# An attention and two MLPs: weight tiles of the second MLP converted in another order, one tile a step, and stores of the first MLP's output issued a step later

## The chip, the cores and the metric

The kernel runs on one core of a Trainium2 chip. The metric is the device time of one execution in microseconds; of several runs the median is taken.

## The reference

Three parts follow each other; all numbers are float32, the weights of the MLPs arrive as float64 words.

```python
scores = q @ k.T / 8 + bias(log1p(|i - j|) / log1p(max(i, 1)))   # 4 batches, 8 heads, 576 x 64
x = softmax(scores) @ v                                          # -> 2304 tokens x 512
h = x @ w_in                                                     # 512 x 2048
x2 = (h - tanh(h)) @ w_out                                       # 2048 x 512
gate = 1 / (1 + exp(-(x2 @ w_gate)))                             # 512 x 1536
out = (gate * (x2 @ w_val)) @ w_out2                             # 1536 x 512
```

## The kernel before

**Precision.** PE multiplies in a reduced float32 format. So each operand is split into a high part (ACT, a cast) and a low part (POOL, the difference), and each product is three: high x high, low x high, high x low.

**Weights.** The class `Weights` (lines 454 to 618) brings each weight tile of 128 x 512 from float64 to a split pair. Its stages: `load` (a DMA into `wraw`, two buffers), `scan` (ACT takes the absolute value of the upper words, L535), `make` (DVE joins the words in four operations, L562, L563, L564, L560) and `split` (ACT's cast, L597, and POOL's difference, L592). The tiles after `scan` are called `wu`. The first 32 items, for the first MLP, stay in SBUF. The others, for the second MLP, are stored to `wsc` in DRAM (`store`, L602) from four staging buffers, and loaded again with each use (`feed`, L802).

**The second MLP's tiles.** Its first two products are computed with seven instead of eight products of 2 x 2 blocks, so four weight blocks `u00`, `u01`, `u10`, `u11` of a group (`fp`, six groups of two blocks of hidden columns) give seven left operands: three are blocks, four are made by the sums of L550, L551, L554 and L555, in place. In the list of items each group has four block tiles, then `c0` and `c1` (the sums, two each, and the splits of what they give), then two tiles of the output weight. That is 6 tiles to convert, 4 sums and 9 splits a group.

**The first MLP.** 48 steps, `n`; 6 blocks of 384 tokens, each visited for the first and later for the second half of the hidden columns, four steps a visit. In step `n` PE runs `first(n)` (24 products `up`, L656) and `fifth(n - 2)` (24 down products into four banks `acc`, L720). Between them lie `second` (ACT: two functions of `up`, L673, and a square, L676), `third` (DVE: five operations, L686 to L690, with one of ACT, L685) and `fourth` (ACT's casts `gh`, L694, and POOL's `gl`, L701). Three steps after a visit's last step `sixth` empties the four banks into `o`: by DVE and ACT in the first visit, by four DVE additions (L736) in the second, and stores them to `x2s` (L740); `partial` (L727) reads them back between. The tokens `xm` of the next block are loaded (L640) and split (`x_split`, L646 and L647) in two of four steps.

**How the conversion is placed.** Nothing schedules it: each engine runs its instructions in the order in which the Python writes them. The loop over `n` (lines 964 on) writes ACT's list `acts`, then runs `third`'s operations and a tile's four conversion operations in turn (`zip_run`), then `sixth`, PE's products, the low parts of the splits, and the next `scan`. For items `c0` and `c1`, where `make` gives two operations, the `while` loop goes on:

```python
            if len(made) != 2:
                break
            run()
            for l in low:
                l()
```

so steps 24, 30, 36 and 42 hold both items and the tile after them. `later` puts a DMA off to the next step's `tick` (in the second MLP to the second slot after): the raw loads and the stores of splits, not those of `x2s`. SP issues all DMAs, in order, and waits at each for what it needs.

**The second MLP.** 252 slots `s` of six matmuls (L848), 14 for a group and pair of token blocks; twelve of the 14 also have a down product of three matmuls (L864). Two banks alternate, so slot `s + 2` waits for the evacuation of slot `s` (L892 to L909, ACT or DVE). Slots 0 to 6 stand in the last two steps of the first MLP's pipeline. The rest of the weight tiles is converted between slots by `convert` (lines 808 to 821), with sums on DVE and three staging buffers. Thirteen buffers hold loaded weights; when the first of a group come free, `feed` issues one load or, in every fourteenth slot, seven.

## Time and profile before

| what | value |
|---|---|
| median of 3 runs (1225.12 to 1227.8) | 1226.7 us |
| profiled execution, its time | 1230.97 us |
| profiled execution, its span | 1229.2 us |
| mean granted clock of PE over the span | 0.97 |
| PE busy | 1137.2 us (93%) |
| DVE, ACT, POOL busy | 814.2, 660.2, 622.5 us |
| shares of the chain that ended last | PE 73%, DVE 7%, DMA 6%, issue 5%, POOL 5%, ACT 4% |

The times are those of the core. The span is the stretch that the profile covers; the execution's own time is a little longer. Times in rows are microseconds from the start of the span. A busy PE is not PE at its peak: its ends are modelled, and at a lower granted clock the same matmuls take longer.

### The profile page before, as it was taken

The page shows a single profiled execution, that of the slowest core. Times are in us where ns is not written, and L with a number is a line of the kernel's source. Part 1 is how long each engine was busy: PE and PEld are TensorE (multiplying, and loading weights), DVE is VectorE, ACT ScalarE, POOL GpSimd, SP SyncE. Part 2 cuts the span into 40 slices and gives each one's busy share as a digit, 9 for nine tenths or more (in the row PEclk, how much of TensorE's full clock was granted, in tenths as well). Part 3 has the DMA queues.
Part 4 walks back from the last instruction along what each step waited for, and adds up shares of the span by engine and source line. Part 5 has one row for each costly group of instructions (what it writes and reads, how often), then busy time and mean ns, then how long its engine had stood idle before and what let it go on. Part 6 is the DMA issues. An engine that isn't in the chain of part 4 may idle for free.

```text
span 1229.2 us, 19862 instructions
## 1 busy us (share of the span) xinstructions
PE 1137.2 (93%) x6968; PEld 993.5 (81%) x6968; DVE 814.2 (66%) x1415; ACT 660.2 (54%) x1313; POOL 622.5 (51%) x574
## 2 busy tenths in 40 slices
PE   5679999999999999988898887987899999999998
PEld 1256676667699999988897887976799999999997
DVE  8978888888489889887779778456625332442222
ACT  7977888887576676765566556232324222332222
POOL 1057777776455555585557644254535232452232
PEclk9989999999999999999898989988899999999999
DMA  6655555453113333454655476487765665466352
GB/s 218 234 170 166 153 157 167 144 170 99 54 59 114 121 120 104 155 208 140 234 181 201 129 251 219 155 316 270 294 258 215 257 239 224 155 256 256 155 218 109
DMA packets 103027, 225.65 MB, mean 184 GB/s; under 512 B 12176, under 2 KB 52368, under 8 KB 102928
## 3 DMA queue, kind: packets, MB, share of 16 engines
q1 hardware_dynamic: 102928, 224.38, 52.4%
q8 instruction: 56, 0.92, 0.3%
q14 instruction: 43, 0.35, 0.1%
HBM read 166.26 MB, written 58.08 MB: 183 GB/s over the span
## 4 chain that ended last, share of the span: by engine, by line
PE 73%; DVE 7%; DMA 6%; issue 5%; POOL 5%; ACT 4%; SPq 0%; DVEq 0%; ACTq 0%; POOLq 0%
PE sum L848 19%; PE acc L720 13%; PE up L656 11%; PE acc L864 7%; PE sc L227 6%; PE pv L319 5%; PE pt L269 5%; PE sum L864 3%; DMA wsc<-w 2%; DMA bsc<-e 2%; POOL w L592 2%; PE bt L75 1%; DMA wraw<-in_wv 1%; PE pv L316 1%; ACT z L673 1%
## 5 line engine op out<-in xcount | busy, mean ns | idle before, releaser
L848 PE MATMUL sum<-w,w 128*128 128x384 f32 x1512 | 309.0, 344 | 22.7 <-DVE t L905 12.1
L848 PEld LDWEIGHTS sum<-w,w 128*128 128x128 f32 x1512 | 276.7, 192 | 46.6 <-DVE t L905 13.4
L720 PE MATMUL acc<-gh,w 128*128 128x384 f32 x768 | 203.5, 347 | 27.0 <-DVE o L736 21.1
L656 PE MATMUL up<-xt,w 128*128 128x384 f32 x1152 | 208.7, 335 | 1.8 <-DVE t L690 1.8
L656 PEld LDWEIGHTS up<-xt,w 128*128 128x128 f32 x1152 | 199.9, 188 | 5.2 <-PE acc L720 2.7
L720 PEld LDWEIGHTS acc<-gh,w 128*128 128x128 f32 x768 | 144.1, 196 | 29.9 <-issue 20.3
L701 POOL TENSOR_TENSOR gl<-t,gh 128x384 fp32r<-128x384 f32 x96 | 103.0, 1093 | 127.2 <-issue 57.3
L259 POOL TENSOR_SCALAR n<-n,rec 128x576 f32<-128x576 f32 x144 | 120.8, 853 | 82.1 <-DVE rec L254 47.6
L592 POOL TENSOR_TENSOR w<-wu,w 128x512 fp32r<-128x512 f32 x86 | 124.6, 1456 | 60.4 <-ACT w L597 48.9
L883 POOL TENSOR_TENSOR gl<-e,gh 128x384 fp32r<-128x384 f32 x54 | 57.1, 1059 | 170.8 <-ACT gh L694 170.8
L720 PE MATMUL acc<-gl,w 128*128 128x384 f32 x384 | 132.4, 345 | 2.3 <-POOL gl L701 2.3
L241 DVE CUSTOM_DVE_ANT_0 n<-sc,bias 128x576 f32<-128x576 f32 x144 | 103.7, 752 | 32.9 <-PE sc L227 22.5
L248 ACT ACTIVATE n<-n,mn 128x576 f32<-128x576 f32 x144 | 111.6, 785 | 7.2 <-DVE mn L241 6.7
L864 PE MATMUL acc<-w,gh 128*128 128x512 f32 x288 | 91.4, 398 | 0.0
L694 ACT CAST gh<-t 128x384 fp32r<-128x384 f32 x114 | 56.5, 515 | 62.3 <-POOL t L920 55.7
L686 DVE TENSOR_TENSOR t<-up,t 128x768 f32<-128x768 f32 x48 | 45.9, 955 | 61.8 <-ACT t L673 61.8
L685 ACT ACTIVATE z<-z,c 128x768 f32<-128x768 f32 x48 | 45.1, 940 | 76.1 <-DVE up L684 76.0
L269 PE MATMUL pt<-ident,n 128*128 128x128 f32 x576 | 80.4, 281 | 1.4 <-ACT at L299 1.3
L909 DVE TENSOR_TENSOR e<-sum,e 128x384 f32<-128x384 f32 x72 | 40.0, 556 | 60.3 <-PE sum L848 60.2
L562 DVE TENSOR_SCALAR wu<-wu 128x512 f32<-128x512 f32 x68 | 54.3, 799 | 38.6 <-ACT wu L535 38.5
L319 PE MATMUL pv<-at,vs 128*64 128x320 f32 (+1 forms) x512 | 79.3, 421 | 0.0
L720 PEld LDWEIGHTS acc<-gl,w 128*128 128x128 f32 x384 | 75.1, 196 | 3.3 <-POOL gl L701 3.3
(110 smaller groups left out, 2054.7 us busy)
## 6 DMA issues: line engine op xcount, KB each, us to landing
w<-wsc SPq DMA_DIRECT2D x162, 512.0 KB, 7.7
wsc<-w SPq DMA_DIRECT2D x54, 512.0 KB, 4.7
wraw<-in_wo SPq DMA_DIRECT2D x28, 512.0 KB, 4.2
bsc<-e SPq DMA_DIRECT2D x36, 295.5 KB, 3.1
xm<-xs SPq DMA_DIRECT2D x48, 192.0 KB, 3.1
x2s<-o SPq DMA_DIRECT2D x48, 192.0 KB, 2.0
wraw<-in_wi SPq DMA_DIRECT2D x16, 512.0 KB, 4.7
wraw<-in_wg SPq DMA_DIRECT2D x24, 256.0 KB, 3.0
```

The lines of the kernel that those rows point to most:

```text
L227: T.matmul(sc[u, t][:, hf, 0:288], q[r, 128 * s:128 * s + 128], k[r, o:o + 288], start=(i == 0), stop=(i == 2))
L241: V.tensor_tensor_reduce(n.rearrange("p (a b) -> p a b", a=2), s[:, :, 0:288], bias[t].rearrange("p (a b) -> p a b", a=2), -0.125, 3.0e38, ...
L248: A.activation(n, n, AF.Exp, bias=m, scale=-1.0, accum_out=nsum[u, t // 4][:, t % 4:t % 4 + 1])
L259: G.tensor_scalar(n, n, nrec[u, t // 4][:, t % 4:t % 4 + 1], 1.0, ALU.mult, ALU.mult)
L269: T.transpose(pt[:, i], n[:, o:o + 128], ident)
L319: T.matmul(p[0][64 * a:64 * a + 64, 0:N], v[:, c - 1, a], main[:, c - 1, a * N:a * N + N], start=False, stop=(c == 4))
L592: self.nc.gpsimd.tensor_sub(w[:, 1], x, w[:, 0].bitcast(F32))
L656: T.matmul(p[:, 0:TB], w[:, a, 128 * kt:128 * kt + 128], x[:, c], start=(kt == 0 and i == 0), stop=(kt == 3 and i == 2))
L701: G.tensor_sub(l, x[:, j], h.bitcast(F32))
L720: T.matmul(ac[blk][d][:, 0:TB], w[:, a, 128 * d:128 * d + 128], c, start=(begin and j == 0 and i == 0), stop=(end and j == NPR - 1 and i = ...
L848: T.matmul(p, w[:, a, o:o + 128], x[:, c], start=(fresh and kp == 0 and i == 0), stop=(kp == 1 and i == 2), skip_group_check=True)
L864: T.matmul(sums[3 * t + d], g[:, c], w[:, a], start=(begin and i == 0), stop=(end and i == 2))
```

## The change

The items `c0` and `c1` go. A table `JOBS` gives, for each of the six tiles of a group, one sum at most and the splits that go with its step; `step` returns them together with the tile's conversion, and the loop takes one `step` per step of the first MLP. The blocks come in another order (`u10`, `u00`, `u11`, `u01`), the four sums are other ones (`s = u00 - u10`, `u10 + u11`, `u10 - u00`, `u01 - u00`, in place), with which `s` stands for one product's operand directly. Sums stand behind the step's splits on POOL, in both MLPs. Conversion begins in step 2 instead of 3, pauses in steps 45 to 47 instead of from 44 on, and goes on from slot 8, with one conversion operation a slot. Slots 0 and 1 stand in step 48 and slots 2 to 6 in step 49, before three and four. The stores to `x2s` go through `later`.

```diff
 STAGE1 = (0, 1, 2, 3)
-CONV2 = 21
 X0_AT = N1 - 4
+X0_STEPS = (X0_AT + 1, X0_AT + 2, X0_AT + 3)
 
...
         for fp in range(NFP):
-            for n in range(2):
-                for k in range(2):
-                    self.items.append((f"u{n}{k}", fp, [col(w, DF2, 2 * fp + n, 2 * k, 2) for w in (wg, wv)]))
-            self.items += [("c0", fp, None), ("c1", fp, None)]
-            self.items += [("p", 2 * fp + j, [row(wo2, 2 * fp + j)]) for j in range(2)]
-        self.raws = [i for i, x in enumerate(self.items) if x[2]]
+            for n, k in ((1, 0), (0, 0), (1, 1), (0, 1)):
+                self.items.append((f"u{n}{k}", fp, [col(w, DF2, 2 * fp + n, 2 * k, 2) for w in (wg, wv)]))
+            self.items += [(f"p{j}", fp, [row(wo2, 2 * fp + j)]) for j in range(2)]
         self.n = len(self.items)
...
-    def fresh(self, i):
-        if i >= RES:
-            self.turns += 1
-        return (self.more if i >= RES and self.turns % 5 > 2 else self.stage[1]).tile([128, 512], F32, name="wu")
+    def fresh(self, k):
+        return (self.more if k in ("u10", "u00") else self.stage[1]).tile([128, 512], F32, name="wu")
 
     def scan(self):
         i = self.scanned
-        if i >= self.n or i - self.done > 1 or (self.items[i][2] and i not in self.raw):
+        if i >= self.n or i - (self.done if i < RES else self.made) > 1 or i not in self.raw:
             return
         self.scanned += 1
         k, f, src = self.items[i]
-        if not src:
-            return
-        u = self.fresh(i)
+        u = self.tmp[i] = self.u[k, f] = self.fresh(k)
         self.nc.scalar.activation(u, self.raw[i][:, :, 1].bitcast(F32), AF.Abs)
-        self.tmp[i] = u
-        if k[0] == "u":
-            self.u[k] = u
 
...
-        k, f, src = self.items[i]
-        if k == "c0":
-            self.u["s"] = self.fresh(i)
-            u, M = dict(self.u), self.mix
-            return [lambda: M.tensor_add(u["s"], u["u10"], u["u11"]),
-                    lambda: M.tensor_sub(u["u10"], u["u00"], u["u10"])]
-        if k == "c1":
-            u, M = dict(self.u), self.mix
-            return [lambda: M.tensor_sub(u["u11"], u["s"], u["u00"]),
-                    lambda: M.tensor_sub(u["u01"], u["u01"], u["u11"])]
...
+    def part(self, x, w, low, at=None):
+        def do_low():
+            self.nc.gpsimd.tensor_sub(w[:, 1], x, w[:, 0].bitcast(F32))
+            low()
+        return (lambda: self.nc.scalar.copy(w[:, 0], x)), do_low
+
     def split(self):
         i = self.done
-        if i >= self.made:
+        if i >= min(self.made, RES):
             return [], []
         self.done += 1
-        k, f, src = self.items[i]
-        if k in "io":
-            parts = [(None, self.tmp.pop(i))]
-        elif k == "p":
-            parts = [((f // 2, GROUPS2 + f % 2), self.tmp.pop(i))]
-        else:
-            self.tmp.pop(i, None)
-            u = self.u
-            parts = {"u00": [(1, u.get("u00"))], "u01": [(2, u.get("u01"))], "u10": [], "u11": [(4, u.get("u11"))],
-                     "c0": [(5, u.get("s")), (7, u.get("u10"))], "c1": [(6, u.get("u11")), (3, u.get("u01"))]}[k]
-            parts = [((f, PRODUCTS.index(j)), x) for j, x in parts]
-        highs, lows = [], []
-        for at, x in parts:
-            if at is None:
-                w = self.out[i] = self.slot(i)
-            else:
-                w = self.slot(self.stages[self.staged % len(self.stages)])
-                self.staged += 1
-
-            def low(at=at, x=x, w=w):
-                self.nc.gpsimd.tensor_sub(w[:, 1], x, w[:, 0].bitcast(F32))
-                if at is None:
-                    self.usable += 1
-                else:
-                    self.later(lambda: self.store(at, w))
-            highs.append(lambda x=x, w=w: self.nc.scalar.copy(w[:, 0], x))
-            lows.append(low)
-        return highs, lows
+        w = self.out[i] = self.slot(i)
+
+        def low():
+            self.usable += 1
+        h, l = self.part(self.tmp.pop(i), w, low)
+        return [h], [l]
+
+    def staged_part(self, key, f, j):
+        w = self.slot(self.stages[self.staged % len(self.stages)])
+        self.staged += 1
+        return self.part(self.u[key, f], w, lambda: self.later(lambda: self.store((f, j), w)))
+
+    JOBS = {0: (None, (("u01", 3), ("p1", 8))), 1: (None, ()), 2: (("s", "u00", "u10", "sub"), (("u00", 1),)),
+            3: (("u10", "u10", "u11", "add"), (("u11", 4), ("s", 7))),
+            4: (("u00", "u10", "u00", "sub"), (("u10", 5), ("u01", 2))),
+            5: (("u01", "u01", "u00", "sub"), (("u00", 6), ("p0", 7)))}
+
+    def step(self):
+        i = self.made
+        if i > self.n or self.scanned <= i < self.n:
+            return [], [], [], []
+        if i == self.n:
+            self.made += 1
+        highs, lows = self.split()
+        conv = self.make()
+        if i <= RES:
+            return highs, lows, [], conv
+        fp, k = divmod(i - RES, 6)
+        mix, parts = self.JOBS[k]
+        fp = fp - (k == 0)
+        for key, j in parts:
+            h, l = self.staged_part(key, fp, GROUPS2 + int(key[1]) if key[0] == "p" else PRODUCTS.index(j))
+            highs.append(h)
+            lows.append(l)
+        mixes = []
+        if mix:
+            o, x, y, op = mix
+
+            def run():
+                if o == "s":
+                    self.u[o, fp] = self.fresh(o)
+                getattr(self.nc.gpsimd, "tensor_" + op)(self.u[o, fp], self.u[x, fp], self.u[y, fp])
+            mixes.append(run)
+        return highs, lows, mixes, conv
 
...
-            nc.sync.dma_start(x2s[128 * d:128 * d + 128, TB * b:TB * b + TB], o[:, 0:TB])
+            W.later(lambda d=d, o=o: nc.sync.dma_start(x2s[128 * d:128 * d + 128, TB * b:TB * b + TB], o[:, 0:TB]))
...
-        while W.done < W.n:
-            if W.done < W.made:
-                highs, lows = W.split()
-                for f in highs + lows:
-                    f()
-            ops = W.make()
-            for f in ops:
+        while W.made <= W.n:
+            highs, lows, mixes, conv = W.step()
+            for f in highs + lows:
+                f()
+            for f in conv:
                 f()
                 yield
+            for f in mixes:
+                f()
             W.scan()
-            if not ops:
+            if not conv:
                 yield
...
-        low, scans, conv = [], 0, []
-
-        def run():
-            for f in acts:
-                f()
-            zip_run(vecs, conv)
-            for x in (acts, vecs, conv):
-                x.clear()
-        while 2 <= n < X0_AT:
-            if W.done < W.made and (W.done < RES or n >= CONV2):
-                h, l = W.split()
-                acts += h
-                low += l
-            made = W.make()
-            conv += made
-            scans += 1
-            if len(made) != 2:
-                break
-            run()
-            for l in low:
-                l()
-            low.clear()
-            W.scan()
-        run()
+        low, mixes, conv = [], [], []
+        if 2 <= n < N1 and n not in X0_STEPS:
+            h, low, mixes, conv = W.step()
+            acts += h
+        for f in acts:
+            f()
+        zip_run(vecs, conv)
+        if n == N1:
+            only1.close()
+            ev = st.enter_context(tc.tile_pool(name="p3e", bufs=6))
+            upst.close()
+            one = st.enter_context(tc.tile_pool(name="ps_w", bufs=1, space=PSUM))
+            four = [one.tile([128, 512], F32, name=f"sum{i}") for i in range(4)]
+            banks = [x[:, 0:TB] for x in four[:2]]
+            sums = four[2:]
+            W.stages = RING[RING_SLOTS:]
+            W.lag = 2
+        for _ in range({N1: 2, N1 + 1: 5}.get(n, 0)):
+            slot2(s)
+            s += 1
         for m in due(n - 1, 2):
             if ends(m):
                 sixth(m)
@@ -1000,28 +996,11 @@
             for _ in first(n):
                 if n < 2:
                     yield
-        elif n == N1:
-            only1.close()
-            ev = st.enter_context(tc.tile_pool(name="p3e", bufs=6))
-            upst.close()
-            one = st.enter_context(tc.tile_pool(name="ps_w", bufs=1, space=PSUM))
-            four = [one.tile([128, 512], F32, name=f"sum{i}") for i in range(4)]
-            banks = [x[:, 0:TB] for x in four[:2]]
-            W.stages = RING[RING_SLOTS:]
-            W.mix, W.lag = V, 2
-            for _ in range(3):
-                slot2(s)
-                s += 1
-        elif n == N1 + 1:
-            sums = four[2:]
-            for _ in range(4):
-                slot2(s)
-                s += 1
         for m in due(n, 2):
             fifth(m)
-        for l in low:
+        for l in low + mixes:
             l()
-        for _ in range(scans):
+        if n < N1:
             W.scan()
...
-        for _ in range(2 if s % SLOTS2 in (0, 2, 7) else 1):
+        if s > SLOTS2 // 2:
             next(conv, None)
```

How the instructions move shows in two places. The first is POOL around step 30, a step with a pair of sums; `w` are staging buffers of splits, `gl` the low parts of the first MLP's activation, `xt` those of its tokens. Before, L550 to L555 being sums and L592 splits:

```order
L701 TENSOR_TENSOR gl<-t,gh 128x384 x2
L550 TENSOR_TENSOR wu<-wu 128x512
L551 TENSOR_TENSOR wu<-wu 128x512
L592 TENSOR_TENSOR w_7337<-wu,w_7337 128x512
L554 TENSOR_TENSOR wu<-wu 128x512
L555 TENSOR_TENSOR wu<-wu 128x512
L592 TENSOR_TENSOR w_7360<-wu,w_7360 128x512
L592 TENSOR_TENSOR w_7361<-wu,w_7361 128x512
L592 TENSOR_TENSOR w_7370<-wu,w_7370 128x512
L592 TENSOR_TENSOR w_7371<-wu,w_7371 128x512
L647 TENSOR_TENSOR xt<-xm,xt 128x384 x2
L701 TENSOR_TENSOR gl<-t,gh 128x384 x2
```

and now, L597 being sums and L547 splits (steps 29, 30 and the beginning of 31):

```order
L701 TENSOR_TENSOR gl<-t,gh 128x384 x2
L547 TENSOR_TENSOR w_7267<-wu,w_7267 128x512
L547 TENSOR_TENSOR w_7268<-wu,w_7268 128x512
L597 TENSOR_TENSOR wu<-wu 128x512
L647 TENSOR_TENSOR xt<-xm,xt 128x384 x2
L701 TENSOR_TENSOR gl<-t,gh 128x384 x2
L547 TENSOR_TENSOR w_7364<-wu,w_7364 128x512
L547 TENSOR_TENSOR w_7365<-wu,w_7365 128x512
L597 TENSOR_TENSOR wu<-wu 128x512
L647 TENSOR_TENSOR xt<-xm,xt 128x384 x2
L701 TENSOR_TENSOR gl<-t,gh 128x384 x2
L547 TENSOR_TENSOR w_7469<-wu,w_7469 128x512
```

Four sums and five splits of one step have become one sum and two splits in each of several steps, and every step's `gl` stands ahead of its splits.

The second is SP around slots 13 to 21 of the second MLP, where raw tiles (`wraw`) stand among loads of weights (`w<-wsc`), stores of splits (`wsc<-w`) and loads of the next tokens (`xt<-x2s`). Before, the first pair of raw loads below being issued in slot 15:

```order
L802 DMA w_9291<-wsc_8_81 128x1024
L802 DMA w_9302<-wsc_0_82 128x1024
L802 DMA w_9316<-wsc_1_83 128x1024
L767 DMA xt<-x2s 128x768
L514 DMA wraw<-in_wg 128x2x256
L514 DMA wraw<-in_wv 128x2x256
L767 DMA xt<-x2s 128x768
L602 DMA wsc_2_102<-w_9338 128x1024
L767 DMA xt<-x2s 128x768 x2
L518 DMA wraw<-in_wo 128x1024 x2
L602 DMA wsc_5_105<-w_9433 128x1024
L602 DMA wsc_4_104<-w_9452 128x1024
```

and now, the raw loads being issued in slots 13, 17 and 21:

```order
L802 DMA w_9304<-wsc_8_81 128x1024
L513 DMA wraw<-in_wo 128x1024
L802 DMA w_9325<-wsc_0_82 128x1024
L602 DMA wsc_5_105<-w_9316 128x1024
L602 DMA wsc_3_103<-w_9317 128x1024
L802 DMA w_9341<-wsc_1_83 128x1024
L767 DMA xt<-x2s 128x768 x3
L513 DMA wraw<-in_wo 128x1024
L767 DMA xt<-x2s 128x768
L602 DMA wsc_4_104<-w_9393 128x1024
L602 DMA wsc_2_102<-w_9394 128x1024
L509 DMA wraw<-in_wg 128x2x256
```

The raw load of slot 15 has moved behind two stores of splits and three loads of tokens, to slot 17.

## Rows read from the trace of the kernel before

**Rows 1.** Windows: stretch, us; busy by engine (x); granted clock; DMA share; GB/s.
```profile
345.53:512.61 167.08, 167.08 (x962) 166.26 (x961) 149.83 (x193) 117.89 (x193) 94.19 (x82) 1.00 0.36 111
512.61:764.87 252.26, 221.09 (x1201) 216.57 (x1199) 199.71 (x244) 146.62 (x239) 149.78 (x126) 0.94 0.56 194
787.55:891.61 104.06, 86.29 (x404) 77.83 (x404) 67.39 (x102) 32.55 (x64) 55.50 (x43) 0.89 0.79 294
```

**Rows 2.** Waits of PE after 330 us: sum, times, longest.
```profile
PE acc L720 <- DVE o L736: 21.1, 4, 8.0
PE sum L848 <- DVE t L905: 12.1, 3, 7.1
...
PE sum L848 <- ACT e L892: 3.7, 1, 3.7
```

**Rows 3.** Timeline, step 30: start, us, instruction, count, [idle before <-releaser].
```profile
575.73 1.29 POOL L550 TENSOR_TENSOR wu<-wu 128x512 f32<-128x512 f32 x1
...
582.67 1.36 DVE L563 TENSOR_SCALAR wu<-wu 128x512 int32<-128x512 int32 x1
584.07 1.63 DVE L564 SCALAR_TENSOR_TENSOR wu<-wraw,wu 128x512 int32<-128x512 int32 x1
585.73 1.64 DVE L560 SCALAR_TENSOR_TENSOR wu<-wraw,wu 128x512 int32<-128x512 int32 x1
587.29 1.94 DVE L736 TENSOR_TENSOR o<-acc,o 128x384 f32<-128x384 f32 x4
...
593.37 0.62 ACT L597 CAST w<-wu 128x512 fp32r<-128x512 f32 x1 [11.16 <-DMA wsc<-w]
```

**Rows 4.** Timeline, a step with one conversion and one split.
```profile
449.96 0.81 ACT L673 ACTIVATE z<-up 128x768 f32<-128x768 f32 x1 [0.77 <-PE up L656]
...
452.01 2.17 POOL L701 TENSOR_TENSOR gl<-t,gh 128x384 fp32r<-128x384 f32 x2 [4.61 <-issue]
...
454.14 1.52 POOL L592 TENSOR_TENSOR w<-wu,w 128x512 fp32r<-128x512 f32 x1
...
457.60 1.05 DVE L690 COPY_PREDICATED t<-z,up 128x768 f32<-128x768 int32 x1
```

**Rows 5.** Timeline, a step whose conversion ran beside a POOL busy throughout.
```profile
532.50 0.94 DVE L686 TENSOR_TENSOR t<-up,t 128x768 f32<-128x768 f32 x1
...
533.69 2.40 POOL L701 TENSOR_TENSOR gl<-t,gh 128x384 fp32r<-128x384 f32 x2
...
534.81 0.41 DVE L563 TENSOR_SCALAR wu<-wu 128x512 int32<-128x512 int32 x1
...
536.01 0.68 DVE L564 SCALAR_TENSOR_TENSOR wu<-wraw,wu 128x512 int32<-128x512 int32 x1
...
537.48 0.92 DVE L560 SCALAR_TENSOR_TENSOR wu<-wraw,wu 128x512 int32<-128x512 int32 x1
...
538.32 1.05 DVE L690 COPY_PREDICATED t<-z,up 128x768 f32<-128x768 int32 x1
```

**Rows 6.** Timeline of PE, the up products of steps 46 and 47.
```profile
742.39 4.33 PE L656 MATMUL up<-xt,w 128*128 128x384 f32 x24
...
756.07 1.20 PE L656 MATMUL up<-xt,w 128*128 128x384 f32 x6
```

**Rows 7.** Timeline of ACT in the second MLP: waits on transfers.
```profile
809.19 0.66 ACT L535 ACTIVATE wu<-wraw 128x512 f32<-128x512 f32 x1 [7.23 <-DMA wraw<-in_wv]
...
841.69 0.66 ACT L535 ACTIVATE wu<-wraw 128x512 f32<-128x512 f32 x1 [9.13 <-DMA wraw<-in_wv]
...
878.18 0.62 ACT L597 CAST w<-wu 128x512 fp32r<-128x512 f32 x1 [5.03 <-DMA wsc<-w]
```

**Rows 8.** Timeline of SP there: the burst of weight loads.
```profile
825.42 4.55 SPq L802 DMA_DIRECT2D w<-wsc  x8
```

**Rows 9.** Chain of waits, undisturbed second MLP: start, us, what.
```profile
982.67 3.14 PE sum L848 x18
1005.87 3.14 PE sum L848 x18
```

More of the change, by code (lines that the diff above doesn't have):

```diff
@@ L479, in __init__ @@
         self.stages = STAGE1
-        self.turns = -1
         self.stored = set()
-        self.mix = nc.gpsimd
         self.clock = self.lag = 0
@@ L505, in load @@
     def load(self):
-        if self.loaded >= len(self.raws):
+        i = self.loaded
+        if i >= self.n:
             return
-        i = self.raws[self.loaded]
         self.loaded += 1
```

## The prediction

> **What bounds the kernel now.** I read the windows first, then the waits of PE, then the timeline around the longest waits. PE is the engine to follow: from 345.53 to 512.61 us, the first half of the first MLP, it is busy for all of 167.08 us at a granted clock of 1.00 (2.4 GHz). That is 20 steps, so 8.35 us a step [rows 1] (a row gives PE, PEld, DVE, ACT and POOL in this order). The next 25 steps (up products from step 23, down products to step 45) take 252.26 us where 25 x 8.35 = 208.9 would do: **43.4 us lost**, part of it as idle PE (221.09 busy), part as slower matmuls (clock 0.94). This is the stretch in which tiles of the second MLP are converted. The list of waits names DVE's `o` additions, 21.1 us in four waits, at most 8.0 [rows 2]. In the second MLP 14 undisturbed slots take 1005.87 - 982.67 = 23.20 us; the two slots without a down product take 3.14 / 3 = 1.05 each, the others (23.20 - 2.10) / 12 = 1.76 [rows 9]. Slots 7 to 55 should then take 7 x 1.05 + 3 x 23.20 = 76.9 us and take 104.06 [rows 1]: **27.2 us lost**, around waits for DVE's and ACT's evacuations [rows 2].
>
> The reader is to see in rows 3 how the first loss arises. Step 30 is one of four (24, 30, 36, 42) in which both sums, five splits and the next tile's conversion stand together. POOL starts the first of four sums at 575.73; DVE's conversion of the next tile waits for a scan that stands on ACT behind the casts of the summed tiles, and its four `o` additions, which free the banks of PSUM, begin only at 587.29; ACT's last split waits 11.16 us for a store to leave its staging buffer, since five splits share four buffers and the stores wait in SP's queue behind the `x2s` stores of the same step. DVE is busy for 149.83 of 167.08 us in the plain steps, 7.5 of every 8.35 [rows 1], so a delay of ten microseconds is worked off at about one per step: the four steps disturb nearly all 25.
>
> **The change, part by part.** *Sums and splits spread over six steps.* A group has the same six conversions, nine splits and four sums as before; only their places change. In a crowded step POOL now has two `gl` subtractions (2.17 together [rows 4]), two splits at 1.52 [rows 4] and one sum at 1.29 [rows 3]: 6.5 us of 8.35. In two steps of four two subtractions for x come on top, priced like the `gl` pair: 8.7, over the step. The mean is 2.17 + 1.09 + (9 x 1.52 + 4 x 1.29) / 6 = 6.4 us. POOL therefore falls behind in single steps by less than a microsecond or, where its operations are stretched (2.40 for the `gl` pair beside DVE [rows 5]), by two or three, and recovers in the two light steps of the six. Its deadline is soft: `gl` ends at 454.2, and PE needs it when it comes to those products some 8.35 us after 449.96, four microseconds later.
>
> DVE keeps four conversion operations and five of the activation in each step. In an ordinary step ACT's square starts at 449.96 and DVE ends at 458.65 [rows 4], 8.7 us later; the up buffer is wanted only half a step after that. In every fourth step DVE then adds four `o` (1.94 us [rows 3]), and the next down products wait for the first: 8.7 + 0.5 - 8.35, about 0.9 us, which no order removes. With the crowding I take 1.7 us for each of the four, 7 us. The x products made in steps 45 and 46 stay as they are, and so does their stall: 756.07 - 742.39 - 8.35 = 5.3 us [rows 6]. For a late `gl`, a scan that waits for POOL's sum in the fourth step of six, or a late raw tile I add 3 us. Of the 43.4 us some 15 stay: **28 us gained**.
>
> *Conversions beside POOL.* In the heavy step the last three conversion operations took 1.36 + 1.63 + 1.64 = 4.63 us beside POOL [rows 3]. Between activation operations, with POOL busy without a pause, the same three took 0.41 + 0.68 + 0.92 = 2.01, and DVE's step from 532.50 to 539.37 lasted 6.87 us [rows 5]. The changed steps are of this second kind, so I price them by rows 5; rows 3 are the upper end. The Trainium skill ("SBUF — State Buffer", section "SBUF: two separate sides") speaks against the change here: it says that VectorE and GpSimd lock a shared pair of ports against each other for a whole instruction. By that rule each conversion operation would sit out a subtraction of POOL, and the sum would be that of the slower rival below. The trace agrees in rows 3 and hardly in rows 5, where what DVE does between two conversion operations gives POOL time to end.
>
> *`x2s` stores a step later.* Twelve groups of four stores move past the raw loads, `xm` loads and split stores of one step. Each is now issued when its data is there, so what stands behind it in SP's queue no longer waits for DVE; their buffers are reused four steps later at the earliest, so nobody waits for the later store. What this is worth lies in the 43.4 us and is not counted again.
>
> *Staging.* Two splits a step wrap four buffers after two steps, 16.7 us; a store is issued one step after its split, which leaves it about 8 us to land. ACT's 11.16 us [rows 3] should not come back in the first MLP.
>
> *First slots.* Two and five instead of three and four slots before the last down products: the same matmuls, nothing counted. Bounds: a microsecond either way.
>
> *The second MLP.* Ten tiles instead of twelve are left, one conversion operation a slot, sums on POOL instead of DVE, the raw tile wanted three slots after its issue instead of one to three. What ends the waits there are transfers: ACT waits 7.23 and 9.13 us for raw tiles and 5.03 us for a store [rows 7]. Half-megabyte pieces at the 294 GB/s of that stretch [rows 1] take 1.78 us. Counted from slot 8 (788.6), the raw tile issued in slot 15 of the old order is piece 11.75, done after 20.9 us, at 809.5; the trace has it at 809.19 [rows 7]. In the new order the tile issued in slot 17 is piece 15.75, done after 28.0 us, while its scan stands at the end of slot 20, 6 x 1.05 + 7 x 1.76 = 18.6 us after slot 8. PE has two slots of slack, to 22.1, and resumes at about 30: this wait grows by some 3 us. The burst of seven loads that SP issues from 825.42 on [rows 8] stands in both orders, and the next raw tile is issued behind it in both: the wait of 7.1 us [rows 2] moves by two slots and stays. The third, 3.7 us [rows 2], becomes about 4.7 by the same count, while some waits of under 1 us go. Together: **2 us lost**; between 8 lost, if ACT's splits wait for stores each time, and 14 gained, if one slot more is enough each time.
>
> **Sum.** 28 - 2 = 26 us. The profiled execution took 1231.0 us (span 1229.2), 4.3 over the median of the runs. So 1205 for such an execution and **1201** for the median.
>
> **The rivals.** *The second MLP's waits go as well.* For it: the raw tiles now come evenly, one each four slots, with no slot that takes two operations. Against it: the count of pieces above, and the bursts. 28 + 14 = 42 us gained: 1185.
>
> *POOL's queue becomes the limit in the crowded steps.* For it: 8.7 us of work in single steps, more if stretched. Then `gl` and the scan behind the sum come late, SP waits for the x subtractions before it can load the next raw tile, and I price this at 1 us on 14 of the 24 steps: 1215.
>
> *Slower: POOL holds DVE up in every step.* Place: the zip of activation and conversion, steps 22 to 44. Price: 4.63 - 2.01 = 2.6 us [rows 3, 5] on 6.87 gives 9.5, with a quarter of the additions' 1.94 about 10.0 a step, 1.6 over 8.35; on 24 steps 39 us, against the 38 (43.4 - 5.3) that the spreading can remove, and 2 to 3 lost later: 1230. It decides once DVE's step passes 9.9 us. Against it: rows 5.
>
> *The change does not do what it says.* The heavy wait could reappear at the staging buffers or at SP, and nothing is gained: 1227. Against it: the eight microseconds that each store has.
>
> **How the numbers follow.** Forecast (own range 1191 to 1211, from 22 to 34 us in the first MLP and 8 lost to 4 gained in the second) 0.61; second MLP as well 0.18; POOL 0.13; DVE held up 0.05; nothing 0.03. The range reaches down to the second case and up to the third: 1185 to 1215. Within 0.2% (2.5 us) is about what a measurement of this kernel cannot tell from no change: 0.03 from the last case; slower 0.05; faster 0.92.
>
> **What would show it.** Right: PE takes about 224 us instead of 252 from the up products of step 23 to the end of the down products of step 45; the waits for `o` fall to about 2 us or less each, but one of 3.5 us stays in step 46; no ACT split waits 11 us in the first MLP; POOL is the same in sum. In the second MLP three waits for transfers remain, at other slots. Wrong: conversion operations of 1.4 to 1.7 us in every step (DVE held up), `gl` among the releasers of PE (POOL), or an undisturbed second MLP.

## The result, and the profile after

The changed kernel takes **1192.1 us** (median; 1188.1 to 1192.6), the kernel before, run beside it, 1227.3: a ratio of 0.970, with a 95% interval of 0.967 to 0.974, so 35 us faster. The forecast was 1201 us with a range of 1185 to 1215. The profiled execution of the changed kernel took 1188.1 us (span 1186.0). It is the shortest of its runs, while that of the kernel before was 3.7 us above its median, so the two traces differ by 43 us, eight more than the medians.

Where the 43 us lie, from the windows after (columns as in [rows 1]): up products of step 23 to the end of the down products of step 45, slots 7 to 55, and the first third of those.

```profile
512.72:732.00 219.28, 212.05 (x1201) 210.28 (x1200) 192.76 (x249) 148.57 (x241) 158.33 (x125) 0.98 0.66 227
753.38:848.40 95.02, 81.32 (x404) 72.52 (x404) 61.07 (x86) 30.37 (x60) 64.01 (x50) 0.98 0.83 310
753.40:785.00 31.60, 27.17 (x140) 24.43 (x139) 22.36 (x31) 11.46 (x24) 23.87 (x18) 1.00 0.96 357
```

The 25 steps took 252.26 us [rows 1] and take 219.28: 33.0 us gained, 24.0 of it idle time of PE (31.2 to 7.2) and 9.0 in matmuls that run at a higher granted clock (221.09 busy to 212.05). Slots 7 to 55 took 104.06 and take 95.02: 9.0 gained, 4.1 of it idle time and 5.0 in the matmuls. The last microsecond lies around the handover between the two MLPs. POOL's busy time in the 25 steps, forecast to stay, rises from 149.78 to 158.33; a sum now takes 1.75 us (row of 626.59 below) where it took 1.29 [rows 3].

PE's waits after 330 us (sum, times, longest):

```profile
PE acc L720 <- DVE o L736: 7.2, 5, 4.1
PE sum L848 <- DVE e L909: 4.3, 1, 4.3
PE sum L848 <- issue: 4.2, 1, 4.2
PE sum L848 <- ACT e L892: 3.6, 2, 3.3
PE sum L848 <- DVE t L905: 3.3, 1, 3.3
```

The 21.1 us for `o` [rows 2] have become 7.2, and 4.1 of these are the one wait of step 46 that was to stay. No `gl` of the first MLP is among the releasers. Three waits of the second MLP remain, at 3.3, 4.3 and 3.3 us, where there were 4.5, 7.1 and 3.7. The up products of steps 46 and 47, on PE's timeline, answer to [rows 6]:

```profile
708.28 4.32 PE L656 MATMUL up<-xt,w 128*128 128x384 f32 x24
723.51 1.72 PE L656 MATMUL up<-xt,w 128*128 128x384 f32 x9
```

They begin 15.23 us apart, 6.9 more than a step takes, and more than the 5.3 before.

A crowded step after the change on DVE and POOL (timeline: start, us, instruction, count, [idle before]):

```profile
620.83 0.96 DVE L686 TENSOR_TENSOR t<-up,t 128x768 f32<-128x768 f32 x1 [1.49 <-ACT t L673]
621.71 0.86 DVE L540 TENSOR_SCALAR wu<-wu 128x512 f32<-128x512 f32 x1
622.49 0.95 DVE L687 SCALAR_TENSOR_TENSOR up<-z,up 128x768 f32<-128x768 f32 x1
623.36 0.41 DVE L541 TENSOR_SCALAR wu<-wu 128x512 int32<-128x512 int32 x1
623.69 0.95 DVE L684 SCALAR_TENSOR_TENSOR up<-z,up 128x768 f32<-128x768 f32 x1
624.55 0.92 DVE L542 SCALAR_TENSOR_TENSOR wu<-wraw,wu 128x512 int32<-128x512 int32 x1
625.39 0.95 DVE L689 SCALAR_TENSOR_TENSOR up<-q,up 128x768 f32<-128x768 f32 x1
626.25 0.92 DVE L538 SCALAR_TENSOR_TENSOR wu<-wraw,wu 128x512 int32<-128x512 int32 x1
627.10 1.05 DVE L690 COPY_PREDICATED t<-z,up 128x768 f32<-128x768 int32 x1
...
621.27 2.18 POOL L701 TENSOR_TENSOR gl<-t,gh 128x384 fp32r<-128x384 f32 x2 [1.75 <-ACT gh L694]
623.41 3.21 POOL L547 TENSOR_TENSOR w<-wu,w 128x512 fp32r<-128x512 f32 x2
626.59 1.75 POOL L597 TENSOR_TENSOR wu<-wu 128x512 f32<-128x512 f32 x1
```

POOL is busy from 621.27 to 628.34, and DVE's nine operations take 628.15 - 620.83 = 7.3 us all the same. This is a step of the kind of [rows 5], not of [rows 3].

### The profile page after: what moved, and what is told of

It is laid out like the page before. It is cut to its first block, busy times and chain, and to the rows that moved or that the text cites. A ratio compares the mean times of both kernels' runs of the same rounds, so it can differ in the third digit from the quotient of the medians.

```text
span 1186.0 us, 19853 instructions
## 1 busy us (share of the span) xinstructions
PE 1128.2 (95%) x6968; PEld 982.6 (83%) x6968; DVE 801.4 (68%) x1407; ACT 660.2 (56%) x1313; POOL 644.5 (54%) x582
## 4 chain that ended last, share of the span: by engine, by line
PE 75%; issue 6%; DMA 5%; POOL 5%; ACT 4%; DVE 4%; SPq 0%; DVEq 0%; POOLq 0%; ACTq 0%
PE sum L848 19%; PE acc L720 13%; PE up L656 12%; PE acc L864 7%; PE sc L227 6%; PE pv L319 6%; PE pt L269 6%; PE sum L864 3%; POOL w L547 2%; DMA wsc<-w 2%; DMA bsc<-e 1%; PE pv L316 1%; PE bt L75 1%; ACT y L62 1%; POOL wu L597 1%
## 5 line engine op out<-in xcount | busy, mean ns | idle before, releaser
L848 PE MATMUL sum<-w,w 128*128 128x384 f32 x1512 | 304.4, 341 | 17.3 <-DVE e L909 4.3
L848 PEld LDWEIGHTS sum<-w,w 128*128 128x128 f32 x1512 | 272.3, 189 | 40.8 <-issue 5.1
L720 PE MATMUL acc<-gh,w 128*128 128x384 f32 x768 | 197.9, 338 | 7.3 <-DVE o L736 7.2
L720 PEld LDWEIGHTS acc<-gh,w 128*128 128x128 f32 x768 | 139.7, 190 | 9.8 <-issue 4.4
L547 POOL TENSOR_TENSOR w<-wu,w 128x512 fp32r<-128x512 f32 x86 | 128.2, 1502 | 33.3 <-ACT w L549 33.3
L720 PE MATMUL acc<-gl,w 128*128 128x384 f32 x384 | 129.4, 337 | 0.0
L241 DVE CUSTOM_DVE_ANT_0 n<-sc,bias 128x576 f32<-128x576 f32 x144 | 103.6, 752 | 32.9 <-PE sc L227 23.0
L647 POOL TENSOR_TENSOR xt<-xm,xt 128x384 fp32r<-128x384 f32 x48 | 49.8, 1056 | 45.0 <-ACT xt L646 44.7
L269 PEld LDWEIGHTS pt<-ident,n 128*128 128x128 f32 x576 | 63.4, 141 | 12.5 <-issue 11.5
```

The costliest lines, as they stand in the source:

```text
L241: V.tensor_tensor_reduce(n.rearrange("p (a b) -> p a b", a=2), s[:, :, 0:288], bias[t].rearrange("p (a b) -> p a b", a=2), -0.125, 3.0e38, ...
L269: T.transpose(pt[:, i], n[:, o:o + 128], ident)
L547: self.nc.gpsimd.tensor_sub(w[:, 1], x, w[:, 0].bitcast(F32))
L720: T.matmul(ac[blk][d][:, 0:TB], w[:, a, 128 * d:128 * d + 128], c, start=(begin and j == 0 and i == 0), stop=(end and j == NPR - 1 and i = ...
L848: T.matmul(p, w[:, a, o:o + 128], x[:, c], start=(fresh and kp == 0 and i == 0), stop=(kp == 1 and i == 2), skip_group_check=True)
```

## The experiments

The theory: the heavy steps 24, 30, 36 and 42 make the loss of the first MLP, since in them DVE's conversion waits for a scan that stands behind four sums of POOL, and the `o` additions stand behind that conversion. The first rival: the queue of SP and the staging buffers make it. For the second MLP: the even pace makes the gain, or the sums off DVE, or the smaller number of tiles.

### The stores alone, on the kernel before

```diff
-            nc.sync.dma_start(x2s[...], o[:, 0:TB])
+            W.later(lambda d=d, o=o: nc.sync.dma_start(x2s[...], o[:, 0:TB]))
```

> The kernel before with one part of the change alone: the four output stores of a block are issued a step later. Theory (the bunched sums and splits of steps 24, 30, 36 and 42 make the loss of the first MLP, and the stores are only a side matter): 25 steps from the up products of step 23 to the end of the down products of step 45 still take 247 to 253 us, and the whole 1222 to 1228. Rival (the stores wait in SP's queue for DVE's additions and hold up the split stores and raw loads behind them): the stretch falls to 235 us or less, the whole to 1210 or less, and ACT no longer waits some 11 us for a staging buffer.

Measured: 1227.4 us against 1231.3, ratio 0.997 (0.995 to 0.998); the 25 steps take 249.0 us, as the theory had it.

### Eight staging buffers, on the kernel before

```diff
-STAGE1 = (0, 1, 2, 3)
+STAGE1 = (0, 1, 2, 3, 4, 5, 6, 7)
```

> The kernel before with eight staging buffers in place of four in the first MLP, all else the same, so that five splits of one step never wait for a store. Theory (three things are bunched in a heavy step: four sums on POOL, the scan behind the casts, and the splits that wait for a buffer; the last is a part only): ACT's waits of some 11 us go, the 25 steps take 232 to 245 us instead of 252, the whole 1208 to 1221. Rival 1 (the staging buffers are all of it): 222 us or less and 1198 or less. Rival 2 (they are beside the path): 250 or more and 1225 or more.

Measured: 1228.0 us against 1231.3, ratio 0.998 (0.996 to 0.999); the 25 steps take 248.6 us. Rival 2 was nearer than the theory's figure. In the kernel before, ACT's list of waits in the 25 steps holds this line, two waits of up to 11.2 us:

```profile
ACT w L597 <- DMA wsc<-w: 21.7, 2, 11.2
```

It is gone in this run and in the run with the stores alone. **21.7 us of waiting were taken away, in two ways, and each gave some 3.5 us.** The prediction had shown that wait as a part of what is bunched in a heavy step; it was hardly what PE stood for. What PE stood for is DVE in step 30 of this same run:

```profile
576.14 1.08 DVE L690 COPY_PREDICATED t<-z,up 128x768 f32<-128x768 int32 x1
580.59 0.90 DVE L562 TENSOR_SCALAR wu<-wu 128x512 f32<-128x512 f32 x1 [3.38 <-ACT wu L535]
581.53 1.37 DVE L563 TENSOR_SCALAR wu<-wu 128x512 int32<-128x512 int32 x1
582.94 1.63 DVE L564 SCALAR_TENSOR_TENSOR wu<-wraw,wu 128x512 int32<-128x512 int32 x1
584.60 1.64 DVE L560 SCALAR_TENSOR_TENSOR wu<-wraw,wu 128x512 int32<-128x512 int32 x1
586.16 1.94 DVE L736 TENSOR_TENSOR o<-acc,o 128x384 f32<-128x384 f32 x4
```

The activation is done at 577.2; 3.4 us go by until the scan, then 5.6 us of conversion in a row beside POOL, and only then come the additions, for which PE waits 7.97 us in this run.

### The sums left out, on the kernel before

```diff
-            self.u["s"] = self.fresh(i)
+            self.fresh(i)
+            self.u["s"] = self.u["u11"]
...
-            return [lambda: M.tensor_add(u["s"], u["u10"], u["u11"]),
-                    lambda: M.tensor_sub(u["u10"], u["u00"], u["u10"])]
+            return [lambda: None, lambda: None]
...
-            return [lambda: M.tensor_sub(u["u11"], u["s"], u["u00"]),
-                    lambda: M.tensor_sub(u["u01"], u["u01"], u["u11"])]
+            return [lambda: None, lambda: None]
```

> The kernel before with the four sums of a group left out everywhere (its summed tiles are then not the sums); loads, conversions, splits and stores all stay. Theory (in a heavy step the chain sums on POOL, casts of the summed tiles, scan of the next tile, its conversion on DVE, o additions makes the loss; the stores and the staging buffers gave 3.6 us each): the 25 steps fall from 252 us to 222 to 234, the waits for o to 3 us or less each. Rival (five splits and stores in one step are enough for it): 242 us or more, and o waits of 6 to 8 us stay.

Measured: 1213.0 us against 1229.2, ratio 0.987 (0.984 to 0.990). The 25 steps take 235.8 us, just over what the theory gave, and the longest wait for `o` falls from 8.0 to 3.7, where the theory had 3 or less. So without the sums half of it is gone: 16.5 of the 33.0 us that the change gained there. The other half is left with the five splits and the conversion in one step; which of these two keeps it this run does not tell.

### The next tile a step later, on the kernel before

```diff
             low.clear()
             W.scan()
+            if W.items[W.made - 1][0] == "c1":
+                break
```

> The kernel before, where a heavy step ends behind its sums: the next tile is converted a step later, so that no activation operation on DVE stands behind a conversion that waits for the sums. Everything is still computed, four tiles later in the second MLP. Theory (DVE's wait inside the heavy step makes the loss): the 25 steps take 222 to 236 us, o waits 4 us or less each; the second MLP then loses 5 to 25 us more, with some sixteen tiles left. Rival (the sums and casts delay gh and gl themselves): 242 us or more.

Measured: 1202.0 us against 1229.2, ratio 0.978 (0.976 to 0.981). **The 25 steps take 218.6 us, the same as in the changed kernel (219.3)** and fewer than the theory's 222 to 236. The four sums are still bunched with three of the five splits, the stores stand where they stood, and the last two splits have moved on with the conversion. But groups now take seven steps, so there are three heavy steps instead of four, and fewer tiles are converted in this stretch (18 times L560, where the kernel before has 21 and the changed kernel 22 of the same operation). That the gain does not come from this alone shows in step 38, which is heavy and has additions:

```profile
642.34 1.29 POOL L550 TENSOR_TENSOR wu<-wu 128x512 f32<-128x512 f32 x1
...
643.88 1.06 DVE L690 COPY_PREDICATED t<-z,up 128x768 f32<-128x768 int32 x1
644.84 1.93 DVE L736 TENSOR_TENSOR o<-acc,o 128x384 f32<-128x384 f32 x4
650.63 0.96 DVE L686 TENSOR_TENSOR t<-up,t 128x768 f32<-128x768 f32 x1 [3.86 <-ACT t L673]
```

The sums begin at 642.34, the additions follow the activation at once, DVE then waits 3.86 us with nothing to do, and PE does not wait at all. What made the loss is the conversion that stood between; to move it, with the two splits behind it, is enough. How much of the equality with the changed kernel is owed to the smaller number of tiles is not shown. The price lies behind: 15 tiles instead of 12 are left over, and slots 7 to 55 take 107.1 us instead of 104.1.

### The stores at once, on the changed kernel

```diff
-            W.later(lambda d=d, o=o: nc.sync.dma_start(x2s[...], o[:, 0:TB]))
+            nc.sync.dma_start(x2s[...], o[:, 0:TB])
```

> The changed kernel with the output stores of a block issued at once again. Theory: with the work spread there is slack in SP's queue, so the 25 steps take 219 to 222 us and the whole 1188 to 1196. Rival (the stores a step later carry a good part of the gain): 228 us or more, 1200 or more.

Measured: 1191.4 us, ratio 0.967 (0.965 to 0.970) to the kernel before; the 25 steps take 218.4 us. The later stores are worth nothing here: some 3.5 us on the kernel before, none once the steps are even.

### Conversion behind the activation, on the changed kernel

```diff
-        zip_run(vecs, conv)
+        for f in vecs + conv:
+            f()
```

> The changed kernel with the four conversion operations of a step behind the five of the activation on DVE in the first MLP, instead of between them. It tests what the alternation does for DVE beside a busy POOL. Theory (activation operations that read PSUM in between give POOL time to end its own): the four operations, now in a row, rise from 2.96 us a step to 4 to 6 us, DVE's step passes 8.35 us in crowded steps, and the whole is 1195 to 1215. Rival (the order of the two does not matter): the four stay within 0.4 us of 2.96 us a step and the whole is 1186 to 1193, since the up buffer is then even released earlier.

Measured: **1237.1 us** against 1231.3, ratio 1.0045 (1.002 to 1.007): the whole gain is gone and a little more. Neither account had that. The rival's time is out by 44 us, the theory's by 22, and the four operations rise less than the theory had, to a mean of 3.2 us a step over the first 21 steps (the sum of the means of their four groups, 0.55 + 0.66 + 0.99 + 0.96) and of 3.5 from 534 to 700 us. But a step as a whole, with POOL at work beside it, goes from 7.3 to 8.7 us (548.22 to 556.91):

```profile
548.22 0.96 DVE L686 TENSOR_TENSOR t<-up,t 128x768 f32<-128x768 f32 x1
549.09 0.95 DVE L687 SCALAR_TENSOR_TENSOR up<-z,up 128x768 f32<-128x768 f32 x1
550.08 0.96 DVE L684 SCALAR_TENSOR_TENSOR up<-z,up 128x768 f32<-128x768 f32 x1
551.14 0.96 DVE L689 SCALAR_TENSOR_TENSOR up<-q,up 128x768 f32<-128x768 f32 x1
552.21 1.07 DVE L690 COPY_PREDICATED t<-z,up 128x768 f32<-128x768 int32 x1
553.17 0.41 DVE L540 TENSOR_SCALAR wu<-wu 128x512 f32<-128x512 f32 x1
553.61 1.15 DVE L541 TENSOR_SCALAR wu<-wu 128x512 int32<-128x512 int32 x1
554.80 1.39 DVE L542 SCALAR_TENSOR_TENSOR wu<-wraw,wu 128x512 int32<-128x512 int32 x1
556.22 0.69 DVE L538 SCALAR_TENSOR_TENSOR wu<-wraw,wu 128x512 int32<-128x512 int32 x1
```

8.7 is over the 8.35 of PE, and the emptying of the four banks stands behind it. PE's waits from 345 to 780 us are these:

```profile
PE acc L720 <- DVE o L736: 22.1, 5, 5.3
PE acc L720 <- DVE o L739: 13.7, 6, 3.5
PE acc L720 <- ACT o L739: 2.4, 1, 2.4
```

They make 38.2 us in twelve waits, one for each of eleven emptyings and a second for the first of them, and that is all the idle time of PE in both stretches. It begins ahead of step 23: the stretch from 345.5 us to the up products of step 23 takes 188.5 us instead of 167.2, and the 25 steps 244.5 instead of 219.3. DVE's slack is thin: 1.4 us more a step turn 35 us of gain into a loss. This is the kind of loss that the prediction's slower rival had, a DVE step over 8.35 us. But the step is 8.7 us long and not 10.0, and 21 of the 46 us lost lie ahead of the steps for which the rival was priced. The alternation of the two kinds of operation is what kept it away.

### The additions earlier, on the changed kernel

```diff
+        if n < N1:
+            vecs[3:3] = [lambda m=m: sixth(m) for m in due(n - 1, 2) if ends(m)]
         zip_run(vecs, conv)
...
-        for m in due(n - 1, 2):
-            if ends(m):
-                sixth(m)
+        if n >= N1:
+            for m in due(n - 1, 2):
+                if ends(m):
+                    sixth(m)
```

> The changed kernel with the four o additions of a block issued between the third and the fourth of DVE's activation operations instead of behind the step's conversion. Theory (the additions stand late on DVE, not on its load): PE's waits for o fall from 7.2 to 2 us or less in sum, the 25 steps take 212 to 216 us instead of 219.3, the whole 1182 to 1188. Rival (DVE is full, the wait moves to the up buffer): 218 to 221 us, with waits for L690.

Measured: 1187.9 us, ratio 0.968 (0.966 to 0.970); the 25 steps take 216.5 us. The four waits of 0.6 to 1.2 us are gone. The wait of step 46 went from 4.1 to 2.9 us, but another of 2.8 us has come up a step later, for a `gh` cast of step 45. That is half a microsecond more than the theory gave at most, and less than the rival. As slots 7 to 55 take 97.9 us in this trace, the whole is not clearly shorter than that of the changed kernel.

### The second MLP: sums, pace and number

```diff
+        self.mix = nc.gpsimd
...
-                getattr(self.nc.gpsimd, "tensor_" + op)(...)
+                getattr(self.mix, "tensor_" + op)(...)
...
-            W.lag = 2
+            W.mix, W.lag = V, 2
```

> The changed kernel with the sums of the second MLP on DVE, as before, instead of POOL. Slots 7 to 55 take 94.9 us in the changed kernel and 103.9 in the kernel before. Theory (the 9 us come from the even pace, which leaves each raw tile three slots to land): 94 to 97 us, the whole 1187 to 1194. Rival (DVE freed of the sums makes them): 100 us or more, the whole 1196 or more.

```diff
-        if s > SLOTS2 // 2:
+        for _ in range(2 if s % SLOTS2 in (0, 2, 7) else 1):
             next(conv, None)
```

> The changed kernel with the pace of the old one in the second MLP: conversions begin in slot 7 and slots 0, 2 and 7 of each fourteen take two operations. Theory (the even pace makes the 9 us of the second MLP): slots 7 to 55 take 99 to 105 us instead of 94.9, the whole 1192 to 1203, with longer waits of ACT for raw tiles. Rival (ten tiles instead of twelve, or the sums, make them): 94 to 96 us, the whole 1187 to 1192.

```diff
-X0_STEPS = (X0_AT + 1, X0_AT + 2, X0_AT + 3)
+X0_STEPS = (X0_AT - 1, X0_AT, X0_AT + 1, X0_AT + 2, X0_AT + 3)
```

> The changed kernel without conversion in two further steps of the first MLP, so that some twelve tiles are left for the second MLP, as before, instead of ten. Slots 7 to 55 take 94.9 us in the changed kernel, 103.9 before; pace and place of the sums changed that by 2 us or less. Theory (the number of tiles that are left makes most of the 9 us): 100 to 106 us, the whole 1193 to 1202. Rival (order of tiles and stores makes it): 94 to 97 us, the whole 1187 to 1193.

Measured, with slots 7 to 55 of the other runs beside them (PE's idle time is the stretch less its busy time; ACT's waits are sums over the stretch):

```
run                 whole, ratio (interval)     slots 7-55  PE idle  PE busy  ACT: raw  ACT: stores
before              1                              104.1      17.8     86.3     20.4       8.1
before_sums_alone   0.978 (0.976 to 0.981)         107.1      17.9     89.1     24.5       3.9
changed             0.970 (0.967 to 0.974)          95.0      13.7     81.3     16.4       1.1
sums on DVE         0.969 (0.968 to 0.971)          96.9      13.3     83.6     15.5       3.6
old pace            0.971 (0.969 to 0.972)          96.1      12.5     83.6     15.8       1.2
twelve tiles        0.970 (0.968 to 0.973)          95.2      12.0     83.2     19.1       0.2
one load a slot     0.966 (0.964 to 0.968)          92.8       8.9     84.0      5.6       4.4
```

Each of the three explanations, taken back alone, costs 0.2 to 1.9 us of the 9. None of them makes the gain; the theories of the runs with the old pace and with twelve tiles failed. For the sums the run that leaves them out of the kernel before agrees: DVE has 60.03 instead of 67.39 us to do in slots 7 to 55, and they take 103.6. The matmuls of the changed kernel's trace (81.3 us) are the fastest of the new order, where the other runs have 83.2 to 84.0; so how the 9 us divide between idle time and matmuls differs from trace to trace. What is common to the runs near 95 and missing in those above 103 is the order of tiles, splits and stores in a group, with two splits at a time, and the places of slots 0 to 6; ACT's waits for transfers are 28.4 or 28.5 us in the two rows with the old order and 17 to 19 in the first four with the new one. That is a conclusion from what is left over. Neither the order nor the places of the slots were tried alone, nor two of the three together, so the cause of these 9 us **stays open** in its parts.

### One ring load a slot, on the changed kernel

```diff
-    def feed():
-        while issued[0] < len(loads):
+    def feed(most=99):
+        last = issued[0] + most
+        while issued[0] < min(last, len(loads)):
...
-        feed()
+        feed(1 if s > SLOTS2 // 2 and W.loaded < W.n else 99)
```

> The changed kernel with at most one ring load issued in a slot from slot 8 on while raw tiles are left to load, so that no raw tile stands behind a burst of them in SP's queue. Theory (the wait of 4.3 us of the changed kernel comes from the burst in front of the raw tile): that wait falls under 1.5 us, slots 7 to 55 take 90 to 93 us, the whole 1184 to 1190. Rival (the transfers are limited by their sum, not by their order): 94 to 97 us, with PE's waits now for ring loads.

Measured: 1185.7 us, ratio 0.966 (0.964 to 0.968); slots 7 to 55 take 92.8 us. In the changed kernel ACT's scans still wait for raw tiles:

```profile
778.56 0.66 ACT L526 ACTIVATE wu<-wraw 128x512 f32<-128x512 f32 x1 [3.27 <-DMA wraw<-in_wo]
...
805.80 0.66 ACT L526 ACTIVATE wu<-wraw 128x512 f32<-128x512 f32 x1 [9.32 <-DMA wraw<-in_wv]
...
831.46 0.66 ACT L526 ACTIVATE wu<-wraw 128x512 f32<-128x512 f32 x1 [3.87 <-DMA wraw<-in_wo]
```

The middle one stood behind the burst, and PE's wait of 4.31 us after it is gone in this run: the theory held for it. Two waits of PE remain:

```profile
PE sum L849 <- ACT e L893: 7.6, 2, 3.9
```

The first, 3.6 us, stands behind the same raw tile as before; ahead of the second ACT waits 3.3 us for a store to leave a staging buffer. Of 4.8 us less idle time 2.2 reach the end of slot 55, because the matmuls took 84.0 us instead of 81.3.

### Both edits together

> The changed kernel with two edits together: at most one ring load a slot while raw tiles are left, and the o additions of a block in the middle of DVE's five activation operations, ahead of all five in the steps that make the x products. Theory (the two gains, 4 and 3 us, lie in different stretches and add up, and the wait of step 46 goes): the 25 steps take 212 to 216 us, slots 7 to 55 take 92 to 94, the whole 1178 to 1184. Rival (what the additions gain is given back in the second MLP, as slots 7 to 55 took 97.9 us in the run with that edit alone): 1184 to 1189.

The edit is that of the two runs, with the additions ahead of all five operations in steps 45 to 47. Measured: **1181.8 us** against 1229.2, ratio **0.962 (0.960 to 0.965)**, faster than the changed kernel. The 25 steps take 216.4 us and slots 7 to 55 take 94.2, both just over what the theory gave, while the whole lies within it. The wait for `o` in step 46 is gone, and one of 3.8 us for a `gh` cast has come up in step 47:

```profile
PE acc L720 <- ACT gh L694: 3.8, 1, 3.8
```

The x products of steps 45 and 46 still stand ahead of the activation on ACT and DVE; here another thing behind them is late.

## Why the prediction was right, and where its sizes were off

**The bound and the place of the loss: right.** The 25 steps and the second MLP are where the time came from, and the waits named there are the ones that shrank.

**The mechanism in the heavy steps: right in its main line, wrong in one link.** That DVE's conversion waits for a scan behind the summed casts, and the additions behind the conversion, is what the run with the next tile a step later shows: with this link undone the 25 steps take 218.6 us, and the additions of step 38 are on time. The link of the staging buffers (ACT's 11.16 us [rows 3]) gave some 3.5 us, with eight buffers as with later stores. The prediction did not price it by itself, so the sum does not suffer.

**What stays in the first MLP: 10.4 us (219.3 - 208.9), forecast 15.** The four waits for additions were taken as 1.7 us each, 7 in sum; they are 0.64, 1.21, 0.69 and 0.62, 3.2 in sum, near the 0.9 that the working had before it added something "with the crowding". The x products were put at 5.3; it is 15.23 - 8.35 = 6.9, and 4.1 of it is one wait. The 3 us for late `gl`, scans and raw tiles are 0.3. So 33 us were gained where 28 were forecast: the crowding terms were too high, by more than the x products were too low.

**Conversions beside POOL: right to take rows 5.** The crowded steps last 7.3 us with POOL busy throughout. The rule of the Trainium skill ("SBUF — State Buffer", section "SBUF: two separate sides"), by which VectorE and GpSimd shut each other out for a whole instruction, would have made it the slower rival. The trace agrees with it where conversions stand in a row beside POOL (1.37 to 1.64 us against 0.41 to 0.69) and hardly where they alternate with operations on PSUM (0.41 to 0.92 us, POOL busy throughout).

**The second MLP: the step that failed.** "2 us lost" was 9 us gained. The sum counted raw tiles by half-megabyte pieces of 1.78 us, at 294 GB/s. That is the mean of a stretch in which the queue also stood still (DMA share 0.79 [rows 1]). In the first third of the same slots it moves 357 GB/s at a share of 0.96, so a piece takes 0.524 MB / 357 GB/s = 1.47 us, and 15.75 of them 23.1; the tile landed 24.2 us after slot 8 (778.56 - 754.4), not 28.0. The wait was 3.3 us, where some 7.5 were forecast. The agreement with the 809.19 of [rows 7] had been taken to bear that price out, and it was luck. From 788.60 to 809.19 the queue of the kernel before hardly stood still: it moved 347 GB/s at a share of 0.98, so a piece took 1.51 us. But the count of 11.75 leaves out four `x2s` stores, 1.5 pieces, that SP issued from 786.78 on, just ahead of slot 8; a count too low and a price too high gave the right end. So one landing fixes neither the count nor the price. The three waits that remain make 10.9 us where there were 15.3, and the prediction had them grow by 4. The second omission: of the 27.2 us lost, only 17.8 were idle time, the rest slower matmuls, and the sum let that rest stand. It fell by 5.0 us in this trace.

**The sum and the range.** 33.0 + 9.0 + 1 stands against 28 - 2. The case "the second MLP's waits go as well" (1185, chance 0.18) came nearer than the forecast: 42 us against the 43 measured in the traces, though three of the waits are still there, only shorter, so its condition did not come true. The median, 1192, lies between the two cases. Both parts of the forecast were too low, by 5 and by 11 us, and did not make up for each other: the first MLP's 33 lies inside its range of 22 to 34, the second MLP's 9 gained lies outside its 8 lost to 4 gained. So the median stands one microsecond inside the forecast's own range, and that owes something to luck.

## What to carry to other kernels

Where an in-order engine does work for the bottleneck and work for later, look at what the later work waits for: one operation that waits puts all that stands behind it late, and moving that one operation out of the step can be worth as much as a new order of everything. The longest wait in a list need not be the one that counts: 21.7 us of ACT's waits were worth some 3.5. And price a queue's transfers by the rate while it is busy, not by the mean of a stretch in which it also stood still, and count all that was issued: one landing that agrees can come from two errors.

## What the hardware showed that was not expected

Alternating two independent chains on DVE is worth more than the durations of its operations tell. The durations of the nine sum up to 8.5 us in a row (548.22 on) and 8.0 in the alternation (620.83 on), but the step takes 8.7 and 7.3. In a row, the five activation operations follow each other by 0.87 to 1.07 us, 4.95 in sum (548.22 to 553.17); in the alternation they hold DVE for 0.86 to 0.88 each and the last for 1.05, 4.5 in sum. The four conversions take 3.7 us in a row and 2.8 in between. Why the dependent operations stand further apart the runs do not show.

Less idle time of PE does not bring a higher granted clock with it. With 13.7 us idle in slots 7 to 55 the row of the changed kernel shows 0.98; with 8.9 us idle the row of the run with one load a slot shows 0.93:

```profile
754.10:846.90 92.80, 83.95 (x404) 75.91 (x404) 59.16 (x87) 30.41 (x60) 63.12 (x50) 0.93 0.85 317
```

Behind the changed kernel's waits of 3.3, 4.3 and 3.3 us PE's next six matmuls take 1.33, 2.12 and 1.33 us, behind the 3.6 and 3.9 us of the other run 2.29 each. The length of a wait alone does not decide it: in the run with the stores at once 2.29 us follow a wait of 2.8 us and 1.33 one of 2.9. No run here separates what does.
